# Output tiles in the freed weight space, and a new planned order, in a gated-recurrence plus spatial-gating kernel

## The chip, the cores and the metric

The kernel runs on one core of a Trainium2 chip. The metric is the device time of one execution in microseconds (us). The engines are TensorE (PE), VectorE (DVE), ScalarE (ACT), GpSimd (POOL) and SyncE (SP); SP issues nearly all transfers. A line number such as L775 is a line of the kernel before.

## The reference, cut to what matters

Two stages follow each other. The first is a gated linear recurrence over 4 batches, 8 heads, 768 steps and a head size of 48; the second is a feed-forward block with a spatial gate, with d_ff = 1024.

```python
for t in range(S):
    state = alpha[:, :, t, :, None] * state + einsum('bhd,bhde->..', k[t], v[t])   # outer product
    y[:, :, t] = einsum('bhd,bhde->bhe', q[:, :, t], state)
x = y.transpose(0, 2, 1, 3).reshape(4, 768, 384)
h = maximum(x @ w_in, 0);  u, v = h[..., :512], h[..., 512:]
v_n = (v - mean(v)) / sqrt(var(v) + 1e-6)
v_s = einsum('ts,bsd->btd', w_spatial, v_n) + b_spatial
out = (u * v_s) @ w_out                                  # (4, 768, 384), float32
```

## The kernel before, in words

**Tiling.** The sequence of each batch is cut into 6 chunks of 128 steps, 24 chunks in all, numbered i = 0 to 23. Chunks 0 to 5 are worked in three pairs (function `pair`), the others singly (function `first`). A single chunk goes through these steps. ACT takes the logarithm of alpha (`la`, L615). PE sums it along the steps (`cum`, L621 and L624). ACT takes the exponentials: `binv` of the negative (L633), `bc` of the sums (L640), and `cum` in place (L650). POOL forms `kt` = k times binv (L645), and DVE forms `qt` = q times the exponential (L655). PE transposes both (`trk`, L672), and ACT or DVE copies the result out (`kqT`, through the copy helper at L207 for ACT and L209 for DVE and POOL). PE multiplies for the scores (`sc`, L702), and DVE masks them in two halves (`m`, tile `ptm`, L713). PE adds the chunk's own part and the part from the state (`y`, L730 and L724). PE also forms the state's update (`upd`, tile `tp`, L688). DVE adds it (`z`, L329), POOL multiplies by bc (`S`, L334), and two casts put it into the block-diagonal tile `sbd` (`sb`), which the next chunk's y reads at L724. ACT casts y (`xs`, tile x_sb), PE transposes it (`xt`, L363), and ACT copies it to `xT` (`xe`).

**Second stage.** It works per batch b with groups of matmuls that all carry L775. `v(b,t)` gives one tile of 128 steps of the half that is normalised: ACT applies the relu, then either DVE takes BatchNorm statistics (L837, L838) or, for the tile pairs named in `ACT_STATS`, ACT takes sums and sums of squares (L822, L833) and DVE makes mean and variance of them with three instructions on two columns (`mv`, L847, L848, L850). ACT makes `rstd` (L859, L860), and DVE normalises (`vn`, L867). `u(b,f,th)` gives the other half, transposed, 384 steps at a time. `s(b,d,th)` multiplies with the transposed w_spatial in two parts of three matmuls, DVE adds the bias (`vsb`, L915), and POOL or DVE multiplies with u (`g`, tile gT, L928, for the last one L911). `o(b,t)` multiplies with w_out in four matmuls, one engine copies the result to SBUF, and SP stores it (L967). An output tile has the number n = 6b + t.

**Where outputs stand.** In `out_tile`, tiles 0 to 7 go into the two `raw_w` buffers in which weights were loaded in float32, tiles 8 to 10 into the three `w_row` buffers, and all others into the pool `outp`, which has four buffers of one tile (`o_sb`).

**What sets the order.** All work is first collected as `Op` objects with engines, planned durations, dependencies and priorities. `schedule` then repeatedly takes the operation that can start first by its own clock (with `PATIENCE` added to the start by kind, and half the duration where there is a choice of engine) and emits it. So the planned durations and waits decide the order on each engine and which engine an operation goes to; on the chip each engine works through its list in that order and waits for semaphores where needed. A load is planned as an issue on SP, a transfer of `LD` and a latency `lat`. In the first 40 us of the plan, where PE would stand idle, filler matmuls on the tile `junk` (L199) are emitted. The stores are issued after the last load.

Of the kernel before, what the change touches and what calls it, by code (L numbers as in the profile page):

```python
# [51 lines left out]
class Clock:  # L52
# [19 lines left out]
        return end  # L72


PATIENCE = {"ev": -0.3, "v": -0.1, "g": -0.3, "sb": 0.3, "bb": 0.5, "ln": 0.2, "z": -0.2, "we": -0.1, "S": 0.2, "cast": -0.1, "rs": 0.1, "trk": -0.1, "xs": -0.3}
ENGINES = {
    "kt": {"POOL": 0.87},
    "vb": {"POOL": 0.47, "ACT": 0.42},
    "S": {"POOL": 0.57},
    "sb": {"POOL": 0.79, "DVE": 0.36},  # L80
    "vn": {"DVE": 0.33},
    "xe": {"ACT": 0.38},
    "ev": {"DVE": 0.61, "ACT": 0.91},
    "u": {"ACT": 0.38, "DVE": 0.47},
    "o": {"ACT": 0.38},
}
PAIRS = (0, 1, 2)
ACT_STATS = ((2, 2), (1, 4), (3, 4))
PIECES = {
    "w_in": ((0, "vc", 0, 0.35), (0, "kc", 2, 0.15)),  # L90
    "w_sp": ((0, "vc", 4, 0.35), (0, "qc", 6, 0.25), (0, "qc", 6, 0.25)),
    "w_out": (0, "qc", 7, 0.25),
}
# [47 lines left out]
def kernel(  # L141
# [14 lines left out]
    B, H, S, D = q.shape  # L156
# [3 lines left out]
    DM = H * D  # L160
# [12 lines left out]
    IO = 3  # L173
    WK = 3
    NB, NKP = 3, 2
    LD, LP, WT, ST = 0.97, 1.46, 2.35, 0.8
    NRAW, NROW, KEEP = 2, 3, 11
    raws = ctx.enter_context(tc.tile_pool(name="raws", bufs=NRAW))
    io_pool = ctx.enter_context(tc.tile_pool(name="io", bufs=IO))
# [111 lines left out]
    def op(key, *args, **kw):  # L291

        users = kw.pop("use", ())
        o = Op(*args, **kw)
        for s in users:
            s.users.append(o)
        ops.append(o)
        made[key] = o
        o.wait = PATIENCE.get(key[0], 0.0)
        return o  # L300

    def got(*keys):
# [87 lines left out]
    def pair(j):  # L390
# [33 lines left out]
        for par in range(2):  # L424
# [42 lines left out]
                    out=ktp[:, par, :, :, 0:D].rearrange("p hp s d -> p (hp s) d"),  # L467
                    in0=st["kc"][:, :, par, :], in1=st[f"binv{par}"])

            op(("ktp", j, par), {"POOL": 0.87, "DVE": 0.47}, None, ktf, got(("einvp", j, par), ("kc", 2 * j)) + tr_users("k", jo), prio=P + 4)  # L470

            def qtf(_, par=par):
                nc.vector.tensor_mul(
# [116 lines left out]
    def first(i):  # L590
# [13 lines left out]

        j = i // 2
        jo = j - NKP
        dma(("ac", i), LD, load("ac", alpha), io_users("ln", j), P)
        dma(("kc", i), LD, load("kc", k), io_users("kt", j), P + 0.1)
        dma(("qc", i), LD, load("qc", q), io_users("qt", j), P + 0.2)
        dma(("vc", i), LD, load("vc", v), io_users("vb", j), P + 0.3)  # L610

        la, kt, qt = [x[j % NKP][:, i % 2].rearrange("p (hp s) d -> p hp s d", s=2) for x in (lap_bufs, ktp_bufs, qtp_bufs)]

# [196 lines left out]
    def second_v(b, tt):  # L810
        mms = [mm(
            lambda ps: ps, lambda ks=ks: bt[b]["xT"][:, ks, tt * 128:(tt + 1) * 128],
            lambda ks=ks: w_in_sb[1][:, ks, :], ks == 0, ks == KS - 1) for ks in range(KS)]
        t0 = tt - tt % 2
        on_act = (b, t0) in ACT_STATS

        def evac(eng, ps):
            d = bt[b]
            if not on_act:
                relu(eng, d["v_sb"][:, tt, :], ps)  # L820
                return
            nc.scalar.activation(  # L822
                out=d["v_sb"][:, tt, :], in_=ps, func=AF.Relu, accum_out=d["sums"][:, 0, tt:tt + 1])

        Q = 1000.0 + 100 * b
        group(("v", b, tt), mms, 0.22, got(("xe", b * NCH + tt)) + made[("w_in", 1)], Q + tt, evac,
              {"ACT": 0.61 if on_act else 0.48}, None, [made.get(("vn", b - 2, tt))], parts=1)

        def bn(_):
            d = bt[b]  # L830
            if on_act:
                sq = small.tile([128, DH], BF16, name="sq", bufs=1)
                nc.scalar.activation(  # L833
                    out=sq, in_=d["v_sb"][:, tt, :], func=AF.Square, accum_out=d["sums"][:, 1, tt:tt + 1])
                return
            stats = small.tile([128, 6], FP32, name="stats")
            nc.vector.bn_stats(out=stats, in_=d["v_sb"][:, tt, :])  # L837
            nc.vector.bn_aggr(out=d["mvs"][:, tt, :], in_=stats)  # L838

        op(("bn", b, tt), {"ACT": 0.65} if on_act else {"DVE": 0.8}, None, bn, got(("v", b, tt)), prio=Q + 10)  # L840
        if tt % 2 == 0:
            return
        two = slice(t0, t0 + 2)
        if on_act:
            def mv(_):
                d = bt[b]
                nc.vector.tensor_scalar_mul(out=d["mvs"][:, two, 0], in0=d["sums"][:, 0, two], scalar1=1.0 / DH)  # L847
                nc.vector.tensor_tensor(  # L848
                    out=d["mvs"][:, two, 1], in0=d["mvs"][:, two, 0], in1=d["mvs"][:, two, 0], op=ALU.mult)
                nc.vector.scalar_tensor_tensor(  # L850
                    out=d["mvs"][:, two, 1], in0=d["sums"][:, 1, two], scalar=1.0 / DH, in1=d["mvs"][:, two, 1],
                    op0=ALU.mult, op1=ALU.subtract)

            op(("mv", b, t0), "DVE", 0.4, mv, got(("bn", b, t0), ("bn", b, tt)), prio=6.0)

        def rs(_):
            d = bt[b]
            r = d["rstd"][:, two]
            nc.scalar.activation(out=r, in_=d["mvs"][:, two, 1], func=AF.Ln, bias=eps_tile)  # L859
            nc.scalar.activation(out=r, in_=r, func=AF.Exp, scale=-0.5)  # L860

        op(("rs", b, t0), "ACT", 0.45, rs, got(("bn", b, t0), ("bn", b, tt), ("mv", b, t0)), prio=6.0)
        for t in (t0, tt):
            def vn(eng, t=t):
                d = bt[b]
                if eng == "DVE":
                    nc.vector.tensor_scalar(  # L867
                        out=d["vn"][:, t, :], in0=d["v_sb"][:, t, :],
                        scalar1=d["mvs"][:, t, 0:1], scalar2=d["rstd"][:, t:t + 1],
                        op0=ALU.subtract, op1=ALU.mult)  # L870
                    return
                nb = small.tile([128, 1], FP32, name="nb")
                nc.gpsimd.tensor_scalar(
                    out=nb, in0=d["mvs"][:, t, 0:1], scalar1=d["rstd"][:, t:t + 1], scalar2=-1.0,
                    op0=ALU.mult, op1=ALU.mult)
                nc.gpsimd.tensor_scalar(
                    out=d["vn"][:, t, :], in0=d["v_sb"][:, t, :], scalar1=d["rstd"][:, t:t + 1], scalar2=nb,
                    op0=ALU.mult, op1=ALU.add)

            op(("vn", b, t), ENGINES["vn"], None, vn,  # L880
               got(("rs", b, t0)) + [made.get(("s", b - 2, x, th)) for x in range(NDS) for th in range(2)],
               prio=Q)
# [13 lines left out]
    def second_s(b, dsl, th):  # L896
# [27 lines left out]
        if last:  # L924
            made[("g", b, dsl, th)] = made[("s", b, dsl, th)]
        else:
            def gm(eng):
                ENG[eng].tensor_tensor(  # L928
                    out=bt[b]["gT"][:, dsl, cols], in0=hold["vs"], in1=bt[b]["uT"][:, dsl, cols], op=ALU.mult)

            op(("g", b, dsl, th), {"POOL": 0.87} if b < B - 1 else {"POOL": 0.87, "DVE": 0.46}, None, gm, got(("s", b, dsl, th)), prio=Q)

    kept = {}

    def out_tile(n):

        if n < 8:
            if n % 4 == 0:
                kept["t"] = raws.tile([128, 4 * DM], FP32, name="raw_w")
            return kept["t"][:, n % 4 * DM:(n % 4 + 1) * DM]  # L940
        if n < KEEP:
            return raws.tile([128, S], BF16, name="w_row", bufs=NROW).bitcast(FP32)
        return outp.tile([128, DM], FP32, name="o_sb")

    def second_o(b, tt):
        mms = [mm(
            lambda ps: ps[:, 0:DM], lambda dsl=dsl: bt[b]["gT"][:, dsl, tt * 128:(tt + 1) * 128],
            lambda dsl=dsl: w_out_sb[:, dsl, :], dsl == 0, dsl == NDS - 1) for dsl in range(NDS)]
        hold = {}
        n = b * NT + tt  # L950
        if n < 8:
            free = [made[("cast", "w_out", x)] for x in range(NDS)] + [made[("cast", "w_sp", 2, x)] for x in range(2)]
        elif n < KEEP:
            free = got(("wt", n - 8 + 3))
        else:
            free = got(("st", (n - 4) // NT, (n - 4) % NT)) if n >= KEEP + 4 else []

        def evac(eng, ps):
            hold["o"] = out_tile(n)
            copy(eng, hold["o"], ps[:, 0:DM])  # L960

        Q = 1000.0 + 100 * b + 30 + tt
        group(("o", b, tt), mms, 0.165, [made[("g", b, x, tt // 3)] for x in range(NDS)] + made[("w_out",)], Q, evac,
              ENGINES["o"], None, free, parts=1)

        def store(_):
            nc.sync.dma_start(out=out[b, tt * 128:(tt + 1) * 128, :], in_=hold["o"])  # L967

        dma(("st", b, tt), ST, store, got(("o", b, tt)), -1.0, issue=0.8)
        if n < KEEP:  # L970
            late.extend((made[("st", b, tt, "issue")], (x, N - 1, "issue")) for x in ("ac", "kc", "qc", "vc"))
        made[("all", b)] = made[("o", b, tt)]
# [104 lines left out]
```

## Time and profile before

| What | Value |
|---|---|
| Median of 5 runs | 155.81 us (155.43 to 155.84) |
| The profiled execution's own time | 155.82 us |
| Its span in the trace | 153.9 us |
| PE, DVE, ACT, POOL busy | 143.7, 123.5, 110.8, 83.7 us |
| Last load lands, first store is issued | 109.5 us, 106.2 us |
| PE's last matmul ends | 148.58 us |
| Last store issued, landed | 150.68 us, 152.81 us |
| Transfers | 28.62 MB, mean 186 GB/s |

The span runs from the first to the last instruction of the program in the trace; the run's own time has 1.9 us more around it. A PE that is busy in the trace is not a PE at its peak, since matmuls overlap and their ends are modelled.

### The profile page before, as it was taken

How to read it: one execution, taken by the hardware profiler on the slowest of the kernel's cores; microseconds unless marked ns; L12 is line 12 of the kernel's file. 1: busy time of each engine (PE TensorE's matmuls, PEld its weight loads, DVE VectorE, ACT ScalarE, POOL GpSimd, SP SyncE). 2: the span in 40 equal slices, each digit the busy share in tenths (PEclk: the TensorE clock that was granted, in tenths of full speed). 3: DMA queues.
4: the chain of work that ended last, by engine and by line, in shares of the span. 5: the costliest groups of instructions: out<-in, count | busy, mean ns of one | idle time of the engine just before them, and what ended most of it. 6: DMA issues, size and time to landing. Idle time of an engine off the chain costs nothing.

```text
span 153.9 us, 4564 instructions
## 1 busy us (share of the span) xinstructions
PE 143.7 (93%) x1746; PEld 95.2 (62%) x1761; DVE 123.5 (80%) x268; ACT 110.8 (72%) x273; POOL 83.7 (54%) x141
## 2 busy tenths in 40 slices
PE   7999799999999999999999999999999989999960
PEld 6597567766657656566557575755666556565530
DVE  7767589589999999996888998899979997367800
ACT  3586486898999596899895779999855848850141
POOL 6738337755337887834389497525658850006300
PEclk9999999999999999999999999999999999999998
DMA  5999999998999989989899999999980013400053
GB/s 119 264 314 289 314 236 259 240 275 169 271 196 236 252 178 218 187 174 205 156 213 197 187 209 206 174 210 216 334 305 4 2 51 109 151 0 2 2 192 119
DMA packets 93015, 28.62 MB, mean 186 GB/s; under 512 B 87872, under 2 KB 91456, under 8 KB 92992
## 3 DMA queue, kind: packets, MB, share of 16 engines
q1 hardware_dynamic: 92960, 28.32, 78.5%
q8 instruction: 14, 0.23, 0.7%
q14 instruction: 9, 0.07, 0.1%
q0 software_dynamic: 32, 0.00, 0.0%
HBM read 23.60 MB, written 4.72 MB: 184 GB/s over the span
## 4 chain that ended last, share of the span: by engine, by line
PE 76%; ACT 6%; DVE 5%; DMA 5%; POOL 2%; issue 2%; ACTq 0%; DVEq 0%; POOLq 0%
PE ps L775 41%; PE pt L672 4%; PE pt L702 4%; DMA out_dram<-o_sb 3%; PE y L363 3%; DMA ac<-in_alpha_dram 2%; PE y L730 2%; PE cum L621 2%; PE tp L688 2%; PE y L573 2%; PE ps L199 2%; PE y L724 2%; POOL gT L928 2%; PE ps L430 2%; PE ps L495 2%
## 5 line engine op out<-in xcount | busy, mean ns | idle before, releaser
L775 PE MATMUL ps<-w_spT,vn 128*128 128x384 bf16 x192 | 36.1, 326 | 0.0
L928 POOL TENSOR_TENSOR gT<-vsb,uT 128x384 bf16<-128x384 f32 x28 | 25.8, 929 | 17.3 <-DVE vsb L915 17.0
L713 DVE TENSOR_TENSOR ptm<-pt,mask 128x512 bf16<-128x512 f32 x36 | 23.5, 681 | 1.7 <-PE pt L702 1.6
L775 PEld LDWEIGHTS <-vn 128*128 128x128 bf16 x192 | 17.1, 97 | 10.2 <-issue 0.2
L645 POOL TENSOR_TENSOR kt<-kc,binv 128x384 bf16<-128x384 f32 x18 | 16.5, 918 | 11.2 <-ACT bc L640 6.2
L334 POOL TENSOR_TENSOR state<-state,bc 128x192 f32<-128x192 f32 x20 | 10.2, 512 | 20.7 <-DVE state L329 12.8
L207 ACT CAST x_sb<-y 128x384 bf16<-128x384 f32 x24 | 11.4, 479 | 10.1 <-PE y L730 7.2
L775 PE MATMUL ps<-w_out_sb,gT 128*128 128x384 bf16 x96 | 18.6, 326 | 0.0
L775 PE MATMUL ps<-xT,w_in 128*128 128x384 bf16 x96 | 18.4, 326 | 0.0
L915 DVE TENSOR_TENSOR vsb<-ps,bsp_bc 128x384 f32<-128x384 f32 x31 | 16.3, 549 | 2.1 <-PE ps L775 1.2
L775 PE MATMUL ps<-w_in,xT 128*128 128x512 bf16 x57 | 16.1, 380 | 1.2 <-ACT xT L207 0.2
L207 ACT COPY o_sb<-ps 128x384 f32<-128x384 f32 x13 | 6.2, 476 | 11.6 <-PE ps L775 9.7
L837 DVE BATCH_NORM_STATS2 stats<-v_sb 128x6 f32<-128x512 bf16 x18 | 12.3, 684 | 1.5 <-ACT v_sb L213 1.4
L213 ACT ACTIVATE v_sb<-ps 128x512 bf16<-128x512 f32 x18 | 10.7, 595 | 3.8 <-PE ps L775 3.4
L207 ACT COPY xT<-y 128x384 bf16<-128x384 bf16 x24 | 11.4, 486 | 1.4 <-PE y L363 1.1
L209 POOL CAST sbd<-state 64x192 bf16<-64x192 f32 x30 | 11.2, 372 | 1.3
L199 PEld LDWEIGHTS <-junk 128*128 128x128 bf16 x112 | 10.3, 108 | 2.1 <-DVE junk L240 1.1
L775 PEld LDWEIGHTS <-gT 128*128 128x128 bf16 x96 | 8.4, 97 | 5.0
L775 PEld LDWEIGHTS <-w_in 128*128 128x128 bf16 x96 | 8.4, 97 | 4.9
L215 DVE TENSOR_SCALAR uT<-ps 128x384 bf16<-128x384 f32 x16 | 8.5, 553 | 3.4 <-PE ps L775 3.3
L867 DVE TENSOR_SCALAR vn<-v_sb,mvs,rstd 128x512 bf16<-128x512 bf16 x24 | 10.5, 472 | 0.8 <-ACT rstd L860 0.7
L775 PEld LDWEIGHTS <-xT 128*128 128x128 bf16 x72 | 6.1, 97 | 6.8 <-ACT xT L207 2.4
(128 smaller groups left out, 314.2 us busy)
## 6 DMA issues: line engine op xcount, KB each, us to landing
ac<-in_alpha_dram SPq DMA_DIRECT2D x18, 192.0 KB, 3.8
kc<-in_k_dram SPq DMA_DIRECT2D x18, 192.0 KB, 4.0
qc<-in_q_dram SPq DMA_DIRECT2D x18, 192.0 KB, 4.0
vc<-in_v_dram SPq DMA_DIRECT2D x18, 192.0 KB, 4.0
out_dram<-o_sb SPq DMA_DIRECT2D x13, 192.0 KB, 2.1
raw_w<-in_moe_w_spatial_dram SPq DMA_DIRECT2D x3, 768.0 KB, 6.1
raw_w<-in_moe_w_in_dram SPq DMA_DIRECT2D x2, 768.0 KB, 8.1
out_dram<-raw_w SPq DMA_DIRECT2D x8, 192.0 KB, 2.6
```

Of the source, the lines that this page charges most:

```text
L199: nc.tensor.matmul(out=flat[:, 0:cols], lhsT=junk[:, 0:128], rhs=junk[:, 0:cols], start=True, stop=True)
L207: nc.scalar.copy(out=out, in_=in_)
L209: ENG[eng].tensor_copy(out=out, in_=in_)
L213: nc.scalar.activation(out=out, in_=in_, func=AF.Relu)
L334: ENG[eng].tensor_tensor(out=st["state"], in0=st["state"], in1=st["bc"][:, :, None].to_broadcast([128, HP, D]), op=ALU.mult)
L645: ENG[eng].tensor_mul(out=kt[:, :, :, 0:D], in0=quad(st["kc"]), in1=st["binv"])
L713: nc.vector.tensor_tensor(out=st["ptm"][:, s], in0=st[f"pt{s}"], in1=mask4, op=ALU.mult)
L775: return lambda ps: nc.tensor.matmul(out=out(ps), lhsT=lhsT(), rhs=rhs(), start=start, stop=stop)
L837: nc.vector.bn_stats(out=stats, in_=d["v_sb"][:, tt, :])
L867: nc.vector.tensor_scalar(out=d["vn"][:, t, :], in0=d["v_sb"][:, t, :], scalar1=d["mvs"][:, t, 0:1], scalar2=d["rstd"][:, t:t + 1], op0=AL ...
L915: nc.vector.tensor_tensor(out=hold["vs"], in0=ps[:, 0:TH], in1=bsp_bc[:, th, :], op=ALU.add)
L928: ENG[eng].tensor_tensor(out=bt[b]["gT"][:, dsl, cols], in0=hold["vs"], in1=bt[b]["uT"][:, dsl, cols], op=ALU.mult)
```

## The change

It has two parts. First, the last four output tiles (n = 20 to 23) go into the `raw_w` space too, so that this space holds twelve tiles in all, eight at a time at most; the very last tile is copied in two halves, one by ACT and one by DVE. Second, the planner's numbers are others: the latency of a load of a single chunk is 3.5 in place of 1.9, several durations are changed (`sb` on DVE from 0.36 to 0.95, `mv` from 0.4 to 0.9, `vn` from 0.33 to 0.42), `S` may go to DVE, `PATIENCE` is changed for some kinds, and single operations get a `NUDGE` on their start. `ACT_STATS` names two tile pairs in place of three, and a piece of w_in and a piece of w_spatial are placed by other rules.

```diff
-PATIENCE = {"ev": -0.3, "v": -0.1, "g": -0.3, "sb": 0.3, "bb": 0.5, ...}
+PATIENCE = {"ev": -0.3, "kt": -0.2, "v": -0.1, "be": 0.2, "sb": 0.3, "bb": 0.2, ..., "xe": -0.2, "y": -0.2}
 ENGINES = {
-    "kt": {"POOL": 0.87},
-    "vb": {"POOL": 0.47, "ACT": 0.42},
-    "S": {"POOL": 0.57},
-    "sb": {"POOL": 0.79, "DVE": 0.36},
-    "vn": {"DVE": 0.33},
-    "xe": {"ACT": 0.38},
+    "kt": {"POOL": 0.9},
+    "vb": {"POOL": 0.48, "ACT": 0.42},
+    "S": {"POOL": 0.5, "DVE": 0.6},
+    "sb": {"POOL": 0.73, "DVE": 0.95},
+    "vn": {"DVE": 0.42},
+    "xe": {"ACT": 0.4},
     "ev": {"DVE": 0.61, "ACT": 0.91},
...
+NUDGE = {
+    ("m", 9, 0): -0.15,
+    ("vn", 0, 4): -0.3,
...
+    ("o", 3, 2, "mm", 0): 0.3,
...
+    ("m", 20, 0): 0.6,
+}
-ACT_STATS = ((2, 2), (1, 4), (3, 4))
+LATE = 3.5
+ACT_STATS = ((2, 2), (0, 2))
 PIECES = {
-    "w_in": ((0, "vc", 0, 0.35), (0, "kc", 2, 0.15)),
+    "w_in": ((0, "vc", 1, 0.35), (0, "kc", 2, 0.15)),
...
-    LD, LP, WT, ST = 0.97, 1.46, 2.35, 0.8
+    LD, LP, WT, ST = 1.03, 1.46, 2.35, 0.8
...
-        o.wait = PATIENCE.get(key[0], 0.0)
+        o.wait = PATIENCE.get(key[0], 0.0) + NUDGE.get(key, 0.0)
...
-        dma(("ac", i), LD, load("ac", alpha), io_users("ln", j), P)
+        dma(("ac", i), LD, load("ac", alpha), io_users("ln", j), P, lat=LATE)
...
-            op(("mv", b, t0), "DVE", 0.4, mv, got(("bn", b, t0), ("bn", b, tt)), prio=6.0)
+            op(("mv", b, t0), "DVE", 0.9, mv, got(("bn", b, t0), ("bn", b, tt)), prio=6.0)
...
-        if n < 8:
+        if n < 8 or n >= B * NT - 4:
             if n % 4 == 0:
                 kept["t"] = raws.tile([128, 4 * DM], FP32, name="raw_w")
             return kept["t"][:, n % 4 * DM:(n % 4 + 1) * DM]
...
+        elif n >= B * NT - 4:
+            free = got(*[("st", 0, x) for x in range(4)])
...
             hold["o"] = out_tile(n)
-            copy(eng, hold["o"], ps[:, 0:DM])
+            if n < B * NT - 1:
+                copy(eng, hold["o"], ps[:, 0:DM])
+                return
+            half = DM // 2
+            copy("ACT", hold["o"][:, 0:half], ps[:, 0:half])
+            copy("DVE", hold["o"][:, half:DM], ps[:, half:DM])
```

The order in which the changed program issues differs from that of before nearly everywhere after the first chunks. The kinds and numbers of PE's matmuls stay the same but for the fillers.

More of the change, by code (lines that the diff above doesn't have):

```diff
@@ L72, in run @@
         return end
-PATIENCE = {"ev": -0.3, "v": -0.1, "g": -0.3, "sb": 0.3, "bb": 0.5, "ln": 0.2, "z": -0.2, "we": -0.1, "S": 0.2, "cast": -0.1, "rs": 0.1, "trk": -0.1, "xs": -0.3}
+PATIENCE = {"ev": -0.3, "kt": -0.2, "v": -0.1, "be": 0.2, "sb": 0.3, "bb": 0.2, "ln": 0.2, "z": -0.2, "we": -0.1, "S": 0.2, "cast": -0.1, "rs": 0.1, "trk": -0.1, "xs": -0.3, "xe": -0.2, "y": -0.2}
 ENGINES = {
-    "kt": {"POOL": 0.87},
-    "vb": {"POOL": 0.47, "ACT": 0.42},
-    "S": {"POOL": 0.57},
-    "sb": {"POOL": 0.79, "DVE": 0.36},
-    "vn": {"DVE": 0.33},
-    "xe": {"ACT": 0.38},
-    "ev": {"DVE": 0.61, "ACT": 0.91},
-    "u": {"ACT": 0.38, "DVE": 0.47},
-    "o": {"ACT": 0.38},
+    "kt": {"POOL": 0.9},
[4 more added lines that the diff above has]
+    "xe": {"ACT": 0.4},
+    "ev": {"DVE": 0.61, "ACT": 0.91},
+    "u": {"ACT": 0.39, "DVE": 0.49},
+    "o": {"ACT": 0.4},
+}
+NUDGE = {
+    ("m", 9, 0): -0.15,
+    ("vn", 0, 4): -0.3,
+    ("qt", 22): -0.3,
+    ("upd", 2): 0.3,
+    ("v", 0, 5): 0.6,
+    ("vbp", 0, 0): -0.6,
+    ("z", 21): 1.5,
+    ("ebc", 0): 0.15,
+    ("ev", "q", 1, 1): 0.15,
+    ("z", 19): -1.5,
+    ("cast", "w_in", 0, 1): -0.15,
+    ("vb", 21): -0.15,
+    ("y", 19): -1.5,
+    ("kc", 0): 1,
+    ("o", 3, 2, "mm", 0): 0.3,
+    ("sc", 1, 0): -0.3,
+    ("tr", "k", 0, 1): -0.3,
+    ("qtp", 0, 0): -0.15,
+    ("y", 2): 0.15,
+    ("xs", 22): -0.3,
+    ("m", 20, 0): 0.6,
 }
 PAIRS = (0, 1, 2)
-ACT_STATS = ((2, 2), (1, 4), (3, 4))
+LATE = 3.5
+ACT_STATS = ((2, 2), (0, 2))
 PIECES = {
-    "w_in": ((0, "vc", 0, 0.35), (0, "kc", 2, 0.15)),
+    "w_in": ((0, "vc", 1, 0.35), (0, "kc", 2, 0.15)),
     "w_sp": ((0, "vc", 4, 0.35), (0, "qc", 6, 0.25), (0, "qc", 6, 0.25)),
@@ L468, in ktf @@
                     in0=st["kc"][:, :, par, :], in1=st[f"binv{par}"])
-            op(("ktp", j, par), {"POOL": 0.87, "DVE": 0.47}, None, ktf, got(("einvp", j, par), ("kc", 2 * j)) + tr_users("k", jo), prio=P + 4)
+            op(("ktp", j, par), {"POOL": 0.9, "DVE": 0.6}, None, ktf, got(("einvp", j, par), ("kc", 2 * j)) + tr_users("k", jo), prio=P + 4)
             def qtf(_, par=par):
@@ L606, in first @@
         jo = j - NKP
-        dma(("ac", i), LD, load("ac", alpha), io_users("ln", j), P)
-        dma(("kc", i), LD, load("kc", k), io_users("kt", j), P + 0.1)
-        dma(("qc", i), LD, load("qc", q), io_users("qt", j), P + 0.2)
-        dma(("vc", i), LD, load("vc", v), io_users("vb", j), P + 0.3)
+        dma(("ac", i), LD, load("ac", alpha), io_users("ln", j), P, lat=LATE)
+        dma(("kc", i), LD, load("kc", k), io_users("kt", j), P + 0.1, lat=LATE)
+        dma(("qc", i), LD, load("qc", q), io_users("qt", j), P + 0.2, lat=LATE)
+        dma(("vc", i), LD, load("vc", v), io_users("vb", j), P + 0.3, lat=LATE)
         la, kt, qt = [x[j % NKP][:, i % 2].rearrange("p (hp s) d -> p hp s d", s=2) for x in (lap_bufs, ktp_bufs, qtp_bufs)]
@@ L929, in gm @@
                     out=bt[b]["gT"][:, dsl, cols], in0=hold["vs"], in1=bt[b]["uT"][:, dsl, cols], op=ALU.mult)
-            op(("g", b, dsl, th), {"POOL": 0.87} if b < B - 1 else {"POOL": 0.87, "DVE": 0.46}, None, gm, got(("s", b, dsl, th)), prio=Q)
+            op(("g", b, dsl, th), {"POOL": 0.9} if b < B - 1 else {"POOL": 0.9, "DVE": 0.69}, None, gm, got(("s", b, dsl, th)), prio=Q)
     kept = {}
     def out_tile(n):
-        if n < 8:
+        if n < 8 or n >= B * NT - 4:
             if n % 4 == 0:
```

## The prediction

> **What bounds the kernel now.** I read the head of the page first, then the chain of waits, then the timelines where the chain leaves TensorE.
>
> ```profile
> span 153.9 us, 4564 instructions
> PE 143.7 (93%) x1746; PEld 95.2 (62%) x1761; DVE 123.5 (80%) x268; ACT 110.8 (72%) x273; POOL 83.7 (54%) x141
> ...
> PE 76%; ACT 6%; DVE 5%; DMA 5%; POOL 2%; issue 2%; ACTq 0%; DVEq 0%; POOLq 0%
> ```
>
> TensorE (PE) is busy nearly throughout and holds 76% of the chain: the kernel is PE's list of work plus the places where the chain leaves it. All sums below are therefore made in PE time. The loads keep the DMA engines busy until 109.5 us, but they run ahead: the kc of chunk 20 lands at 96.1, and its transposes (L672) run at 110.9.
>
> Three places matter. At 74 us, from the chain of waits over 70 to 80 us (start, length, what):
>
> ```profile
> 74.42 0.53 DVE mvs L847
> ...
> 74.98 0.41 DVE mvs L848
> ...
> 75.69 0.30 ACT rstd L859
> ...
> 77.46 0.91 ACT kqT L207
> 78.38 0.05 issue
> 78.42 0.40 PE pt L702 x8
> ```
>
> Three tiny VectorE (DVE) instructions (L847 to L850) hold up rstd, ScalarE (ACT) stands behind rstd in its order, and the kqT copy that PE's L702 needs comes late. At 122 us, the same view over 112 to 126 us:
>
> ```profile
> 121.72 1.24 DVE vn L867 x2
> 122.96 0.47 DVE sbd L209
> ...
> 123.45 0.40 DVE sbd L209
> ...
> 123.90 0.34 PE y L724 x4
> ```
>
> PE has nothing from about 123.07 (its previous matmuls, issued from 122.42, need 0.65) until 123.90: 0.83 us. At the end, the chain over 140 to 154 us:
>
> ```profile
> 144.88 0.49 ACT o_sb L207
> 145.37 0.02 issue
> 145.38 4.21 DMA out_dram<-o_sb
> ...
> 149.70 0.96 ACT o_sb L207 x2
> ```
>
> and PE's timeline there:
>
> ```profile
> 145.17 3.41 PE L775 MATMUL ps<-w_out_sb,gT 128*128 128x384 bf16 x20
> ```
>
> PE is finished at 148.58, but the fifth output copy waits for the first of four o_sb buffers to be stored. The last store is issued at 150.68 and lands at 152.81; 1.1 us of closing semaphores follow.
>
> [...]Here 13 o_sb stores take 1.8/2.1/4.2 us[...] and the 4.21 above is an outlier to explain. [...]the same sbd cast on DVE takes 240 to 593 ns.[...]
>
> **The change, part by part.**
>
> *1. Last four outputs in the weight space.* The copies of o(3,2) to o(3,5) no longer wait for stores: nothing else uses that space then (the stores that read it land by 113.4). PE's last six groups are now o(3,0), s, o(3,1), o(3,3), o(3,4), o(3,5), o(3,2), where before o(3,2) stood ahead of o(3,3). o(3,3) needs the last gT (L911: starts 145.44, 0.558, so ready near 146.05), and o(3,1) ends at 145.17+4×0.163 = 145.82: PE now waits **0.25**, which o(3,2) covered. The last copy is a whole 0.48 us ACT copy of o(3,2), since only o(3,5) is split in halves. The copies kept 0.65 apart (146.02, 146.67, 147.32), so the sixth starts at 148.62 when PE ends at 148.58. It ends at 149.10, is issued at 149.12 and lands, at 2.1, at 151.2 instead of 152.81: −1.6. But the first store of this burst landed 4.2 us after issue, the next three only 0.47 apart behind it (149.60, 150.08, 150.55, 151.01), and SP's third issue took 1.46. If that repeats, stores five and six land at about 151.5 and 152.0: −0.8. I take the middle, **−1.2** (bounds −1.6 and −0.5). SP has nothing else queued there.
>
> *2. What leaves DVE.* Ten sbd casts go to POOL (10×0.363 = 3.6 off DVE), seven uT copies to ACT (7×0.553 = 3.9), one stats group of two tiles comes back from ACT (+2×(0.684+0.182) = 1.7, less one group L847–L850 of 0.86), three state products (L334) come from POOL, for which DVE has no row (page 0.36, POOL's own 0.51: I take 0.5 each, 1.5), the rest (−0.62 kt, −0.54 w_spT, +0.68 and +0.42 kqT, +0.33 half copy) +0.3. Together DVE loses about 5 us of 123.5, POOL gains 10×0.372+2×0.509+0.508+0.915−3×0.512 = 4.6 on 83.7, ACT loses about 1. PE loses nothing. These shares buy no time by themselves; what counts is the waits they end.
>
> *3. Waits of before that the new order takes away.* (a) sb.20 is on POOL right behind S.20, ahead of kt.21, no longer behind two vn: −0.83. (b) batch 1's tiles 4 and 5 take BatchNorm stats on DVE: no mvs group there, no square pass ahead of xT on ACT; the two PE waits of that place (v on chunk 12's xT at 75.20, 0.39; L702 at 78.42, 0.28) go: −0.67. (c) batch 3's tiles 4 and 5 lose their square passes on ACT too (L833, 0.64+0.20 each), so no square pass and no o_sb copy stands ahead of chunk 23's xT there; the 0.26 for which PE waited before the v at 133.5 goes. Sum **−1.76**, bounds −1.76 and −0.8 (what is late next at (a) is the mask product m.21.1, with 0.2 us to spare by the same rows).
>
> *4. Waits that the new order brings.* The order in which each built program issues its instructions is known. I laid the old trace's PE durations (v 0.65, u and half an s 0.487, o 0.65, cum 0.263, transposes 0.447, upd 0.241, scores 0.329, y 0.375, xt 0.167) along both orders, counted the PE work between each producer and its consumer, and compared it with what the rows need. x transposes to v need 0.73 (chunk 21: 125.61 to 126.34): the new order leaves 0.58 for chunk 6 and 0.59 for chunk 10, +0.29. cum to transposes needs 0.25+0.50 (binv) +0.1+0.92 (kt) +0.1 = 1.87; chunk 11 gets 1.67: +0.20. Products after scores need 1.45 (L702 ends 114.74, two ptm end 116.13, plus 0.06); the tightest are 1.46 and 1.47: nothing. Sum **+0.49**. What in-order queues add beyond this I cannot read off: the old order had about 1 us in waits under 0.12 each and a few singles; I add **+0.4** (−0.5, if most of that 1 us goes, to +1.5).
>
> *5. The start.* The filler matmuls on junk (L199) rise from 20,896 to 22,560 columns; 18 of 192 took 1.56 us in the chain, 0.087 each, so that is 0.75 us. Chunk 6's cum, transposes, update and scores move behind y.4, y.5 and v(0,5); between y.5 and v(0,4) PE now has only xt.4 and xt.5, where sc.6 and wt.2 (0.33+0.335) worked. m.2.1 stands behind an mvs group (0.86) that waits for two ACT square passes, so y.4 may be later. Against it, waits of 0.46, 0.14 and 0.28 at 35 to 39 us go. I take **+0.6** (0 to 1.2).
>
> *6. Loads.* SP's order is unchanged but for the third w_spatial piece one load later (behind qc.8) and, from chunk 18, alpha and v ahead of k and q. kc.20 comes about three loads (3 us) later against 14.8 us of margin: nothing. The larger planned latency moves no transfer itself. [...]by PE work chunks 15, 17, 18 come 4 to 6 later, inside the margin.
>
> *Sum.* PE's end: +0.6 −1.76 +0.49 +0.25 +0.4 = −0.02; tail −1.2. Against the profiled run's own 155.82 (span 153.9 and 1.9 around it; the median is 155.81, so no correction) this is 154.6.
>
> **The rivals.** *A, POOL becomes the releaser of PE (slower).* POOL takes ten more sbd casts, and kt, S, sb and g stand in one queue. For it: POOL waited 12.8 us for DVE's state, so each S waits in front of kt. Against it: 54% busy, 70 us idle in the trace. It decides where kt ends later than the PE work between cum and transposes covers (1.7 to 4.2 us in the new order); if two thirds of the ten casts' 3.7 us come to stand there, that is +2.5: 157.1; slower from +1.5 on. *B, the store burst sets the end.* The first store's 4.2 us repeats or worsens, worth −0.5 only: 155.3. *C, no new waits,* start at 0, tail −1.6: 154.6 −0.4 −0.6 −0.4 = 153.2. *D, the tail's gain is spent on PE,* whose end slips by 1.2: 155.8; the change then moves the end of PE, not the end of the kernel.
>
> **How the numbers follow.** A measurement of this kernel can tell about 0.2%, 0.3 us. Chances: forecast (154.0 to 155.1) 0.40, C 0.18, B 0.15, D 0.10, A 0.17. Faster is forecast, C and B, 0.73; same D, 0.10; slower A, 0.17. From C's 153.2 to 156.4, where the milder half of A lies, leaves out about 2 in 10.
>
> **What would show it.** Right: no o_sb wait on a DMA, last store issued near 149.1 with PE ending at 148 to 149; no mvs group near 75 us, no wait of L724 on a DVE sbd; a PE wait of about 0.25 before o(3,3). Wrong: PE ending after 149.7 with kt or state of POOL as releasers (A); an unchanged landing near 152.5 with the last copy at 149 (B).

## The result, and the profile after

The changed kernel takes **156.06 us** (median of 43 runs) where the kernel before takes 155.66 us (80 runs). The ratio is **1.0035, 95% interval 1.0024 to 1.0046**: slower by 0.4 us between the medians and 0.5 by the ratio, where 154.6 was predicted. The profiled execution took 156.01 us with a span of 154.2 us, against 155.82 and 153.9.

The head of the page after, and the shares of its chain of waits:

```profile
span 154.2 us, 4566 instructions
PE 144.6 (94%) x1750; PEld 96.0 (62%) x1768; DVE 119.5 (77%) x256; ACT 111.8 (72%) x270; POOL 87.7 (57%) x152
...
PE 82%; ACT 4%; DMA 4%; issue 3%; DVE 2%; POOL 1%; SPq 1%; DVEq 0%
```

The busy times of DVE and POOL moved about as worked out (4.0 us less and 4.0 more, where about 5 and 4.6 were predicted); ACT gained 1.0 where it was to lose about 1. PE has more of the chain. Time did not follow. The end, from the chain over 144 to 155 us and PE's timeline there:

```profile
143.99 5.75 PE ps L799 x34
...
149.76 0.48 ACT raw_w L231
```

```profile
146.31 3.41 PE L799 MATMUL ps<-w_out_sb,gT 128*128 128x384 bf16 x20
```

No output copy waits for a store any more. But PE ends at 146.31 + 3.41 = 149.72, which is 1.14 us later than before (148.58). The last store lands at 153.12 (before 152.81), so from PE's end to that landing it takes 3.40 us where it took 4.23. The span's +0.3 is +1.14 from PE and −0.83 from this tail (the time from PE's end to the last landing). Rival D ("the tail's gain is spent on PE") had the first of these right (1.2), but not the second.

To see where PE lost it, I follow its **lag**: the start of an operation minus the durations (those of the prediction's step 4) of all real PE operations that stand ahead of it in that kernel's order. A wait makes the lag grow, and kernels of different order can be compared at the same amount of work done. The second row is after minus before:

| Time in the after kernel, us | 35 | 40 | 48 | 57 | 65 | 74 | 82 | 90 | 99 | 108 | 116 | 125 | 133 | end |
|---|---|---|---|---|---|---|---|---|---|---|---|---|---|---|
| Difference of lag, us | 0.06 | 0.73 | 0.59 | 1.21 | 0.98 | 1.17 | 0.76 | 0.75 | 1.52 | 1.76 | 1.91 | 2.11 | 1.18 | 1.14 |

The start costs 0.73. After it the falls (48, 65, 82, 90, 133, end) sum to −1.76 and the rises to +2.17. This split hangs on the points chosen, and single points on how the two orders are matched, by 0.2 to 0.4; what is firm is the end and so the net +0.41 after the start. The two places that the prediction showed in the kernel before are indeed free. The chains over 73 to 80 us and 120 to 126 us hold PE alone at those places, among others:

```profile
75.78 0.20 PE y L754 x8
75.98 0.98 PE ps L799 x6
76.96 0.45 PE pt L696 x8
```

```profile
124.00 1.62 PE ps L799 x10
125.62 0.17 PE y L748 x4
```

The y that takes the state (L748, formerly L724) follows the group ahead of it at once. In their place stand new waits. Three of them, from the chain of waits (start, length, what). At 37 us the transposes of chunk 5 wait for the cast of x, with nothing put between:

```profile
36.81 0.29 PE y L603 x4
37.10 0.02 issue
37.12 0.49 ACT x_sb L231
...
37.66 0.34 PE y L387 x3
```

At 90 us DVE works through vn, vsb and state before the kqT copy (L233), and PE's L726 waits for that:

```profile
90.02 0.27 DVE vn L891
...
90.34 0.54 DVE vsb L939
90.89 0.27 DVE state L353
91.15 0.61 DVE kqT L233
...
91.80 0.39 PE pt L726 x7
```

The group sc.15 should have followed at 91.39; seven of its eight matmuls start at 91.80, 0.41 later. The queue may not have made that wait alone: of the two vn ahead of this chain's vsb, the first took 1.12 us beside two gT products on POOL and the second 0.40 with POOL idle, 0.72 more than the second and more than the wait; no run tests this. At 100 us ACT has a square pass, a relu, an exponential and an output copy ahead of the exponential of chunk 18 (L674):

```profile
99.89 0.62 ACT sq L857
...
100.52 0.58 ACT v_sb L237
101.10 0.38 ACT binv L657
101.48 0.43 ACT w_row L231
101.91 0.39 ACT cum L674
...
102.33 0.56 DVE qt L679
...
102.91 0.18 ACT bc L664
...
103.14 0.34 PE y L748 x4
```

That costs PE 0.28. Others are 0.36 before y.8 at 54.88, and several of 0.1 to 0.2.

### The profile page after: what moved, and what is told of

The parts are those of the page before. It is cut to its first block, busy times and chain, and to the rows that moved or that the text cites. A ratio compares the mean times of both kernels' runs of the same rounds, so it can differ in the third digit from the quotient of the medians.

```text
span 154.2 us, 4566 instructions
## 1 busy us (share of the span) xinstructions
PE 144.6 (94%) x1750; PEld 96.0 (62%) x1768; DVE 119.5 (77%) x256; ACT 111.8 (72%) x270; POOL 87.7 (57%) x152
## 4 chain that ended last, share of the span: by engine, by line
PE 82%; ACT 4%; DMA 4%; issue 3%; DVE 2%; POOL 1%; SPq 1%; DVEq 0%
PE ps L799 47%; PE pt L696 6%; DMA qc<-in_q_dram 4%; PE pt L726 3%; PE y L387 3%; PE cum L645 2%; PE y L754 2%; PE tp L712 2%; PE y L597 2%; PE y L748 2%; PE y L223 2%; PE ps L519 2%; PE ps L809 2%; PE ps L223 1%; PE pt L570 1%
## 5 line engine op out<-in xcount | busy, mean ns | idle before, releaser
L861 DVE BATCH_NORM_STATS2 stats<-v_sb 128x6 f32<-128x512 bf16 x20 | 13.7, 684 | 5.2 <-ACT v_sb L237 5.0
L799 PE MATMUL ps<-w_in,xT 128*128 128x512 bf16 x54 | 15.3, 380 | 1.4 <-issue 0.4
L237 ACT ACTIVATE v_sb<-ps 128x512 bf16<-128x512 f32 x20 | 11.9, 597 | 6.0 <-PE ps L799 5.0
L358 POOL TENSOR_TENSOR state<-state,bc 128x192 f32<-128x192 f32 x17 | 8.7, 513 | 11.9 <-DVE state L351 7.4
L233 POOL CAST sbd<-state 64x192 bf16<-64x192 f32 x40 | 13.8, 344 | 2.3 <-DVE state L358 0.6
L223 PEld LDWEIGHTS <-junk 128*128 128x128 bf16 x119 | 10.9, 107 | 2.1 <-DVE junk L264 1.1
L891 DVE TENSOR_SCALAR vn<-v_sb,mvs,rstd 128x512 bf16<-128x512 bf16 x24 | 11.7, 517 | 0.2
L231 ACT COPY o_sb<-ps 128x384 f32<-128x384 f32 x9 | 4.3, 482 | 9.9 <-PE ps L799 9.9
L237 ACT ACTIVATE uT<-ps 128x384 bf16<-128x384 f32 x23 | 10.7, 488 | 0.4 <-PE ps L799 0.4
L679 DVE TENSOR_TENSOR qt<-qc,cum 128x384 bf16<-128x384 f32 x18 | 9.8, 548 | 0.8 <-ACT cum L674 0.6
```

The source lines that it names most:

```text
L223: nc.tensor.matmul(out=flat[:, 0:cols], lhsT=junk[:, 0:128], rhs=junk[:, 0:cols], start=True, stop=True)
L231: nc.scalar.copy(out=out, in_=in_)
L233: ENG[eng].tensor_copy(out=out, in_=in_)
L237: nc.scalar.activation(out=out, in_=in_, func=AF.Relu)
L679: nc.vector.tensor_mul(out=qt[:, :, :, 0:D], in0=quad(st["qc"]), in1=st["cv"])
L799: return lambda ps: nc.tensor.matmul(out=out(ps), lhsT=lhsT(), rhs=rhs(), start=start, stop=stop)
```

## The experiments

Ratios are to the kernel before, run beside each kernel on the same chip. Operations carry the names of the code: sc.15 is the scores group of chunk 15.

**1 and 2. The two parts of the change, each alone.** `e1_tail_only` is before with the output part, `e2_order_only` is after without it.

```diff
 # e1, on before
-        if n < 8:
+        if n < 8 or n >= B * NT - 4:
...
+            copy("ACT", hold["o"][:, 0:half], ps[:, 0:half])
+            copy("DVE", hold["o"][:, half:DM], ps[:, half:DM])
 # e2, on after: the same lines taken back
```

> The kernel before with the output part alone (last four outputs in the weight space, last tile in halves); planner numbers and hence the order on every engine as before. Theory M (the two parts work against each other: the output part gains about what it gained in the profile of after, 0.83 us between PE's last matmul and the last landing, and the new order costs PE 1.14 us): PE ends near 148.6 as before, the last store lands 3.3 to 3.6 us later, time 0.7 to 1.2 us under before (ratio 0.992 to 0.996). Rival S (the store burst sets the end, so the output part is worth little): within 0.3 us of before. Rival R (the reused space itself delays PE): PE ends over 0.5 us later.

> The changed kernel with outputs placed as before (last four in o_sb, no halves); the order on PE, DVE and POOL is that of after. Theory M: PE ends near 149.7, the fifth copy waits for a store again, time 0.9 to 1.4 us over before (ratio 1.006 to 1.009). Rival O (the order costs nothing, and the later PE end in the one profile of after is chance or comes from the output part): within 0.3 us of before.

Measured: e1 154.89 us, ratio **0.9968** (0.9942 to 0.9994); e2 156.77 us, ratio **1.0079** (1.0051 to 1.0107). The product is 1.0047, the whole change 1.0035: the parts add up. The output part gains about 0.5 us (0.1 to 0.9 by its interval, in the mean a little short of theory M's 0.7 to 1.2), the order loses about 1.2. In e1 every engine has the order of before, PE ends at 148.62 (before 148.58), and the halves lie at the end as planned (ACT's at 148.66, DVE's at 149.01).

In e2, PE ends at 149.98, 1.4 us later than before; of that, 0.26 is there against after by 34 us, in the same order on PE.

**3. The planned latency alone taken back.** `e4_old_latency` is after with one number changed.

```diff
-LATE = 3.5
+LATE = 1.9
```

> The changed kernel with the planned load latency at 1.9 as before (all else of after kept). The order changes from PE's 152nd entry on: chunk 6 stands again ahead of y.4 and between y.5 and v(0,4). Theory M with the latency as cause of the loss at the start (0.62 us by 42 us): that part goes, PE ends 0.4 to 0.8 us earlier than in after, time 155.3 to 155.7 unless new queue waits come in. Rival L (loads really land late, so an order that counts on early loads makes PE wait): PE waits of over 0.5 us between 40 and 60 us, time 156.3 or more.

Measured: 158.29 us, ratio 1.0185 (1.0156 to 1.0215). Its lag is 0.4 above that of before at 39.5 us, but 1.26 by 45 us and 4.06 at the end. Taking the larger latency away made the order worse by 2.2 us against after. The time is the one that rival L gave, but its waits of over 0.5 us between 40 and 60 us are not in the trace: the large ones stand at 36.7 us (0.9, before y.4), 76 (1.0), 131 (0.6) and 138 (0.75). Neither theory holds as written. The edit plans everything behind chunk 6 anew, so it doesn't price the late place of chunk 6 by itself.

**4. Three planned durations alone.** `e5_small_ops` is before with planned times of small DVE operations nearer to its trace, where the two casts of an `sb` took 0.50 to 0.94 us together (mean 0.73), the three instructions of an `mv` 0.48 to 1.17 (mean 0.86), and a `vn` 0.38 to 1.01 (median 0.41, mean 0.47).

```diff
-    "sb": {"POOL": 0.79, "DVE": 0.36},
-    "vn": {"DVE": 0.33},
+    "sb": {"POOL": 0.79, "DVE": 0.95},
+    "vn": {"DVE": 0.42},
...
-            op(("mv", b, t0), "DVE", 0.4, mv, ...
+            op(("mv", b, t0), "DVE", 0.9, mv, ...
```

> The kernel before with the planned times of three kinds of small VectorE ops alone raised (sb on VectorE 0.95, mv 0.9, vn 0.42); latency, ACT_STATS and outputs as before. Theory M (waits at 75, 78 and 123 us come from these numbers): they go, 1.3 us in all, and some come in elsewhere; time 0.3 to 1.0 us under before. Rival Q (any reshuffled order trades old queue waits for as many new ones): within 0.4 us of before.

Measured: 156.54 us, ratio **1.0075** (1.0046 to 1.0104). The lag is +0.64 against before by 34 us, +1.9 at 83, +3.0 at 121 and +2.0 at the end. Of the first 0.64, 0.33 is there by 18 us, ahead of the first change in order, and so isn't the order's (see the last section). About 1 us comes back where before has its waits, but more has been lost by then. Neither theory gave this time: M said 0.3 to 1.0 us faster, Q the same within 0.4.

**5. One wait taken away, all else left alone.** `f1_state_cast` is e1 with one operation moved in the finished plan; PE, ACT and POOL have the order of before.

```diff
 # DVE's order
-z.21 s.2.2.1 vn.3.0 vn.3.1 sb.20 bn.3.2
+z.21 s.2.2.1 sb.20 vn.3.0 vn.3.1 bn.3.2
```

> The kernel before with the output part, and one operation moved by hand: the DVE cast sb.20 stands ahead of the two vn instead of behind them; PE, ACT and POOL have the order of before. Theory W (a single wait taken away in an order that is otherwise left alone reaches the end of PE): the 0.83 us for which PE stood before L724 near 123 us goes, nothing else changes, PE ends near 147.8 instead of 148.6, the time is 0.8 under that of the output part alone (154.9), so near 154.1, ratio to before 0.991 to 0.993. Theory X (a wait that is taken away is paid again a little later, since the chains of the other engines stand right behind it): PE still ends within 0.3 us of 148.6, ratio 0.995 to 0.998.

Measured: **153.88 us, ratio 0.9886** (0.9846 to 0.9925), the best of all kernels here. From the chain over 118 to 124 us:

```profile
121.37 1.73 PE ps L794 x9
123.10 0.17 PE y L743 x4
```

The 0.83 us are gone. In the trace the lag against e1 falls by 0.65 (from −0.17, there since before 34 us, to −0.82), because the scores group sc.23 now waits 0.28 where it waited 0.08. Theory W holds here: what is not paid back at the next operation reaches the end. The ratio is better than W's 0.991 to 0.993, and the gain on e1 by the two ratios (0.8%, some 1.3 us) is larger than the 0.65 that the traces place; with 6 runs the intervals leave room for that, and the rest isn't explained.

**6. Two more waits taken away by hand.** `f2_and_stats` is f1 with further moves on DVE and ACT.

```diff
 # DVE
-mv.1.4 u.1.1.1 qt.13 z.13 vn.1.4
+u.1.1.1 qt.13 z.13 mv.1.4 vn.1.4
 # ACT
-bn.1.5 xe.12 eexp.13 rs.1.4 v.2.0 u.1.2.1 u.1.3.1 ev.13
+xe.12 eexp.13 bn.1.5 v.2.0 u.1.2.1 rs.1.4 u.1.3.1 ev.13
```

> The former kernel, and at 72 to 78 us the three mv instructions of tile pair (1,4) moved behind qt.13 and z.13 on DVE, and on ACT xe.12 and eexp.13 ahead of the last square pass, rstd behind one uT copy; PE and POOL keep the order of before. Theory W: the two PE waits of that place (0.39 and 0.28) go as well; PE ends near 147.2, time near 153.5, ratio 0.986 to 0.990. Theory X: what is won at 75 us is lost again by 90 us, so that the time is that of the former kernel within 0.3 us.

Measured: 154.63 us, ratio 0.9945 (0.9925 to 0.9966), 0.75 us slower than f1. Of the two old waits (0.16 and 0.28 in the trace of e1) the first is gone; for the second the chain over 75 to 82 us shows a larger one:

```profile
76.56 0.36 DVE state L354
...
77.30 0.30 DVE mvs L875
...
77.62 0.30 ACT rstd L884
...
78.06 0.47 ACT uT L237
78.53 0.91 ACT kqT L231
...
79.49 0.40 PE pt L727 x8
```

The mv instructions now stand behind `z`, which waits for PE's update. On ACT, rstd waits for them, and uT and kqT stand behind rstd; sc.13 waits 0.92. Against e1, the lag has grown by 0.47 across 72 to 83 us. Another +0.56 was there before 34 us already, where the orders of the two are the same and PE's matmuls ran slower up to about 10 us (a pair took 0.82 us where e1 has 0.50, last section). So 0.47 of the timed 0.75 is placed. Neither theory foresaw a loss.

**7. Two of the new waits taken away in the changed kernel.** `s1_mid`, with PE and POOL in the order of after.

```diff
 # DVE
-vn.2.1 s.1.2.1 z.15 ev.16 S.15      and   mv.2.2 bn.2.4 qt.18
+vn.2.1 ev.16 s.1.2.1 z.15 S.15      and   bn.2.4 qt.18 mv.2.2
 # ACT
-bn.2.3 v.2.4 einv.18 o.1.4 eexp.18 o.1.5 ebc.18
+v.2.4 einv.18 eexp.18 ebc.18 bn.2.3 o.1.4 o.1.5
```

> The changed kernel with five operations moved by hand and the same PE and POOL order: on DVE the kqT copy ev.16 ahead of the vsb and z that stood before it, and mv.2.2 behind qt.18; on ACT eexp.18 and ebc.18 ahead of two output copies and of the square pass bn.2.3. Theory W: the new waits before sc.15 (0.41) and before y.17 (0.28) go and nothing comes for them; PE ends near 149.0 instead of 149.7, time near 155.4, ratio to before 0.997 to 1.000. Theory X: the lag falls by 0.4 at 92 us and is back by 110 us; PE ends within 0.2 of 149.7, ratio 1.002 to 1.005.

Measured: 155.93 us, ratio 1.0028 (1.0007 to 1.0049), not to be told from the changed kernel's 1.0035. The kqT copy runs at 90.25 instead of 91.07, and the 0.41 before sc.15's matmuls is gone. Then, in DVE's timeline of s1:

```profile
91.69 0.91 DVE L381 TENSOR_TENSOR state<-state,bc 128x192 f32<-128x192 f32 x1
92.52 1.27 DVE L760 TENSOR_TENSOR ptm<-pt,mask 128x512 bf16<-128x512 f32 x2
```

and in DVE's of after:

```profile
91.67 0.42 DVE L358 TENSOR_TENSOR state<-state,bc 128x192 f32<-128x192 f32 x1
```

The state product takes 0.91 instead of 0.42. In s1, vsb came later, and with it POOL's gT, which ran until 92.38, over the first 0.69 us of the product (in after it ended at 91.87, 0.20 into the product). The masks came later, and PE waited 0.46 in and behind sc.16. At 103 us the old wait of 0.28 before y.17 is gone as well, and within a microsecond xt.17 waits 0.43 for a cast of x on ACT, which now stands behind what was moved ahead. The lag against after was −0.09 at 90 us, −0.36 at 103 and +0.05 from 108 on. Theory X holds here.

**8. The kernel before, profiled again.** No edit.

> The kernel before, unchanged, profiled a second time. If the 4.2 us of the first store of the last burst belongs to the kernel, it comes again, the fifth output copy waits for a DMA for about 0.5 us or more, and the last landing is 4.2 us after PE's end. If it belongs to the one execution, that store lands after 1.8 to 2.3 us, and PE's end to the last landing takes 3.5 to 3.9 us; then only about 0.5 to 0.9 us were to be had from the tail.

Measured: 156.16 us for the one run. From the chain over 144 to 155 us:

```profile
145.74 4.30 DMA out_dram<-o_sb
...
150.14 0.95 ACT o_sb L207 x2
```

The long first store comes again. It belongs to this kernel in both of its profiles. From PE's end to the last landing it takes 4.21 us.

**9 to 12. A planned number changed by little.** `r1_xe`, `r2_state` and `r3_late_only` are made from before, `r4_after_kt` from after.

```diff
 # r1
-    "xe": {"ACT": 0.38},
+    "xe": {"ACT": 0.4},
 # r2
-    "S": {"POOL": 0.57},
+    "S": {"POOL": 0.5},
 # r3: the four loads of a single chunk
-        dma(("ac", i), LD, load("ac", alpha), io_users("ln", j), P)
+        dma(("ac", i), LD, load("ac", alpha), io_users("ln", j), P, lat=3.5)
...
 # r4, on after
-    "kt": {"POOL": 0.9},
+    "kt": {"POOL": 0.87},
```

> The kernel before with one planned duration changed by 0.02 us: xe on ACT from 0.38 to 0.40. No instruction is added or taken away, the fillers are the same; by the planner's clock 63 of PE's operations from v(2,0) on stand in another order, with the like on the other engines. Theory N (each reshuffle brings new waits of its own size, whatever its inputs say): the time moves by 0.3 to 1.5 us, slower more likely than faster; near 156.3, ratio 1.002 to 1.010. Theory M (an order only gets slower where the planner's numbers get worse; 0.40 is nearer to the 0.44 to 0.50 of the trace): 155.2 to 155.8, ratio 0.997 to 1.001.

> The kernel before with one planned duration changed: S on POOL from 0.57 to 0.50, which is the chip's own 0.51; 109 PE operations change places. Theory N: time moves by 0.3 to 1.5 us, more likely slower, ratio 1.002 to 1.010. Theory M: a truer number gives the same or a better order, ratio 0.995 to 1.001.

> The kernel before with the planned latency of single-chunk loads at 3.5 instead of 1.9 and nothing else. Theory N: ratio 1.002 to 1.015, with a lag of about 0.5 us that appears at 35 to 42 us (chunk 6 stands later, fillers rise from 20,896 to 22,048 columns) and waits of new places later. Theory M (later loads are nearer to what the chip does, so waits for data go): ratio 0.995 to 1.000.

> The changed kernel with one planned duration changed by 0.03 us: kt on POOL from 0.90 back to 0.87; 94 PE operations from cum.9 on change places, fillers and start are those of the changed kernel. Theory N: time moves by 0.3 to 1.5 us against the changed kernel's 156.0, here in either direction, since its order has 2 us of waits to lose; ratio to before 0.996 to 1.012. Theory M: 155.8 to 156.3, ratio 1.002 to 1.005.

| Kernel | PE operations in another place | us | Ratio | 95% interval |
|---|---|---|---|---|
| r1_xe | 63 | 156.26 | 1.0064 | 1.0038 to 1.0090 |
| r2_state | 109 | 154.95 | 0.9994 | 0.9969 to 1.0019 |
| r3_late_only | 108 | 156.19 | 1.0067 | 1.0040 to 1.0094 |
| r4_after_kt | 94 | 164.11 | **1.0588** | 1.0537 to 1.0640 |

Moving one planned duration by 0.02 us cost 0.6%, and by 0.03 us some 5.5%; the instructions' kinds and numbers on PE are the same but for r3's fillers. Theory M is out by r1, which brings a planned number nearer to the trace (the xT copies of before took 0.47 to 0.53 us) and is slower. r2 brings one nearer too (S on POOL took 0.51 in the mean) and is the same. r3 doesn't test M, since its premise is not shown: in before, the loads of a single chunk landed 3.8 to 4.0 us after the start of their issue (medians by tensor), where the planner's issue, transfer and latency make 0.99 + 0.97 + 1.9 = 3.86 us, and 5.46 with 3.5. Theory N holds for r1 and r3, missed r2 (no change), and was far too mild for r4. There, the chain over 71.5 to 74.6 us has

```profile
71.62 0.42 ACT la L639
...
72.09 0.32 PE cum L645
...
73.49 0.39 ACT cum L674
```

ACT reaches the logarithm of chunk 12 (la, L639) at 71.6 only, behind rstd, a relu, a kqT copy and two uT copies; PE's cum waits 0.66 and y.11 another 1.75, and up to sc.12 the lag grows by 1.14 more. Chunks run late from there on. At 138 to 147 us chunk 23's scores, masks, cast and transposes follow each other one at a time with nothing left to put between, and PE loses 5.2 us more.

Not all of this is waiting. The stretches view of r4 (start and end, length, busy time and instructions of PE, PEld, DVE, ACT and POOL, then granted clock and DMA) has

```profile
75.42:78.84 3.42, 2.79 (x29) 1.76 (x29) 1.72 (x3) 1.61 (x5) 1.19 (x3) 0.50 1.03 208
...
143.69:147.10 3.41, 3.41 (x11) 1.51 (x11) 0.88 (x2) 1.50 (x4) 0.00 (x0) 0.50 0.00 0
```

Twice, shortly behind some 3 us in which PE was busy for less than half (1.29 of 3.00 from 72.0, 1.41 of 3.60 from 140.0), the granted clock stood at half for 3.4 us. The 12 matmuls from 144.53 take 3.39 us, the same 12 in after (from 135.54) 2.11. An estimate from these figures: half of the 3.41 us, 1.7 us, of the 5.2 and at most half of the 2.79, 1.4 us, of the earlier loss are the clock's. This profile is of the slowest of r4's six runs (165.84 us); three of them have a mean clock of 0.979, the three faster ones 0.989. No profile of another kernel here has such a stretch between 11 us and PE's end; their mean clocks are 0.993 to 1.000, and one such stretch would take 0.011 off (1.7 of 154 us). So r4's 5.5% is a price of waits and of the clock together, and not what a reshuffle costs by its waits alone.

## Why the prediction was wrong, point by point

**The start (step 5): right.** Predicted +0.6, measured +0.73, of which 0.06 was there by 35 us. One of its waits was named (y.5 to v(0,4) with only xt.4 and xt.5 between: 0.57 at 37 us).

**The waits removed (step 3): right in place, too large in size.** Predicted −1.76. At the places named the lag falls by 0.93 (125 to 133 us, where (a) and (c) claimed 1.09) and 0.41 (74 to 82 us, where (b) claimed 0.67): −1.34. Two of the four waits were smaller than they looked. The trace of before holds 57 of the 72 matmuls of the v groups, that of e1, with the same order on every engine, all 72. First before, then e1, in PE's timeline:

```profile
75.20 0.59 PE L775 MATMUL ps<-w_in,xT 128*128 128x512 bf16 x2 [0.23 <-ACT xT L207]
...
133.48 0.59 PE L775 MATMUL ps<-w_in,xT 128*128 128x512 bf16 x2
```

```profile
75.01 0.82 PE L775 MATMUL ps<-w_in,xT 128*128 128x512 bf16 x3
...
133.29 0.82 PE L775 MATMUL ps<-w_in,xT 128*128 128x512 bf16 x3
```

The three matmuls of a v group start 0.22 us apart. In before the first has no record, and its time was counted as a wait. In e1 the v at 75.01 waits 0.16 (not 0.39) and the one at 133.29 waits 0.03 (not 0.26). The four waits were 0.83, 0.16, 0.28 and 0.03, in all 1.30: what was there went. That all falls of the table sum to −1.76 is chance. Experiment 5 shows the mechanism of (a) by itself.

**The waits brought (step 4): the step that failed most.** Predicted +0.49 and +0.4, in all 0.89. Measured is the net +0.41 after the start; with the 1.30 removed, the order brought **+1.71**. (The rises of the table less its small falls, 2.17 − 0.42, say nearly the same.) I had compared the PE work between producer and consumer with the time that one chain of operations needs, as if each engine took up an operation once its inputs are there. The new waits shown have their cause in what stands ahead in the queue of ACT or DVE: kqT behind vn, vsb and state; the exponential of chunk 18 behind a square pass and an output copy. "What in-order queues add beyond this I cannot read off" was the honest sentence, and +0.4 was the wrong size for it. With its upper bound, +1.5, step 4 would have been 1.99.

**The wait of 0.25 before o(3,3) (step 1): absent.** The last gT runs from 146.58 to 147.14 in after, and PE's 20 matmuls from 146.31 on have no gap. A group of o takes gT in four pieces; only the fourth matmul needs the last one.

**The tail (step 1): −0.83 in the profiled pair, not −1.2.** The sixth store was issued at 150.27 and took 2.85 us, the fifth 2.3; the four ahead took 1.86 to 1.9. I asked whether before's 4.2 us belongs to the one execution: it doesn't (experiment 8). But it doesn't belong to the old placement either. From PE's end to the last landing, the old output part takes 4.23 and 4.21 us in before, yet 3.48, 2.99, 3.85, 2.93 and 3.39 in e2, e5, r1, r2 and r3. The new one takes 3.40 in after and 2.99, 3.01, 2.94, 2.52, 2.52 and 2.51 in e1, f1, f2, s1, e4 and r4. The means are 3.58 and 2.84, a difference of 0.7, but over different orders. Pairs with the same order give −1.23 (before, e1) and −0.08 (e2, after), and s1, which ends like after, takes 0.9 less than after. So single profiles don't fix what the placement is worth; the timed runs say 0.5 (e1). Why the first store is long in before alone stays open.

**The sum.** PE's end: −0.02 predicted, +1.14 measured. Of the 1.16 between them the start has +0.13, step 3 +0.46 and step 4 +0.82, and the 0.25 that didn't come takes off as much. The tail adds +0.37. Together 1.5 us: 154.6 would have been 156.1, and 156.06 was measured. **Rivals:** A fell (the new waits shown come from ACT and DVE, not from kt or state on POOL, though POOL's gT may have a hand in the one at 90 us), B and C fell. C's 153.2 took off only the 0.4 of step 4, where "no new waits" would take off the 0.49 and 0.25 as well. D had a chance of 0.10 and came nearest (155.8); it had PE's slip right and the tail's gain too large.

Experiments 3, 4 and 9 to 12 add a reason to weigh the new waits more. Of seven other orders that the planner gave (after's counted by e2, then e4, e5, r1 to r4), none was faster than that of before by more than its interval, one was equal and the others lost 0.6% or more. What the input of a planner says about single operations did not tell the direction. This was not known from the profile; that a whole new order brings waits at new places could have been.

## What to carry to other kernels

A wait removed by planning everything anew can be paid for with waits that nobody has seen yet, here 1.7 us for 1.3. To forecast a new order, walk the queues of all engines in their order and not only PE's distances; where that can't be done, the new waits may be as large as those removed, and not near zero. Before a gap is counted as a wait, see whether all matmuls of the group ahead of it and behind it have a record. And where only one or two waits are worth something, moving those operations by hand and keeping the rest is worth a try: one moved cast and the output placement gave 0.9886 where the new plan gave 1.0035. It isn't safe either: of the three kernels with moves by hand, this one kept its gain, and in the other two (experiments 6 and 7) what was won came back as a wait a little later.

## What the runs showed of the hardware that I had not expected

The product of two float32 SBUF tiles on DVE (128x192, the state times bc) took 0.36 us with POOL idle (after, 122.75 us). Where a gT product of POOL covered its first 0.20, 0.48 and 0.69 us it took 0.42 (after, 91.67), 0.70 (after, 56.51) and 0.91 (s1, 91.69): it ended about 0.22 us behind POOL's product each time. In s1 that is 0.49 us more than in after, on PE's path. A vn (L891) took 1.12 us beside two gT products on POOL (after, 88.97) and 0.40 with POOL idle (90.02). So in these rows a DVE operation took 0.06 to 0.72 us longer with a gT product of POOL beside it, while the planner takes its duration as fixed; why it does is not shown.

Five executions with the same orders on PE at the start (before twice, e1, f1, f2) differed in PE's lag at 34 us by up to 0.73 us. All of it is there by 18 us, and the largest part comes from PE's first matmuls: in f2 the pair at 6.64 us (128x384 each) takes 0.82 us where e1 has 0.50, and the four transposes at 9.59 take 0.63 where e1 has 0.40; from 10.69 on both have 0.39. e5 and r4 have such a lag too, +0.33 against before and +0.61 against after by 18 us. A pair of single profiles can't attribute less than that to an edit unless the lag grows at a place that can be named. In the pair of the result it is 0.06 at 35 us.

In the last burst a store of 192 KB took 1.84 to 4.3 us. Which stores are long differs from kernel to kernel; in before the first was the longest twice (4.21 and 4.30).
